# Scores, state update and state product of an mLSTM stage as float32 matmuls on two heads per 128 rows

## The chip, the cores and the metric

The kernel runs on one core of a Trainium2 chip. The metric is the device time of one execution in microseconds (us). The engines are TensorE (PE, with its weight loads PEld), VectorE (DVE), ScalarE (ACT), GpSimd (POOL) and SyncE (SP), whose queue issues nearly all transfers.

## What is computed

Three layers follow one another on 4 x 768 = 3072 tokens: an mLSTM recurrence with 8 heads of 40 numbers, a first dense layer of 2048 features with a leaky unit, and a second layer in which each token goes through one of 8 experts of 1024 features. All results are float32.

```python
for t in range(S):                                    # mLSTM, per batch and head
    m_new = np.maximum(f_gate[:, :, t] + m, i_gate[:, :, t])
    f_stab = np.exp(f_gate[:, :, t] + m - m_new); i_stab = np.exp(i_gate[:, :, t] - m_new)
    C = f_stab * C + i_stab * np.einsum('bhd,bhe->bhde', vt, kt)
    n = f_stab * n + i_stab * kt
    h_tilde = np.einsum('bhde,bhe->bhd', C, qt)
    denom = np.maximum(np.abs(np.einsum('bhd,bhd->bh', n, qt)[:, :, None]), 1.0)
    y[:, :, t] = o * h_tilde / denom                  # o = sigmoid(o_gate)
h = x @ w_in                                          # first layer, x is y with heads joined: 320 wide
x = (np.maximum(h, 0) + alpha * np.minimum(h, 0)) @ w_out
# second layer: expert_idx = argmax of normalised logits, then for each expert e
out[mask] = gate_w[mask, None] * (np.maximum(x[mask] @ w1[e], 0) @ w2[e])
```

## The kernel before

**The mLSTM works on 24 chunks** of 128 tokens (4 batches of 6). For each chunk `i` the kernel forms the scores of its tokens with each other (`a_s`, L433), weights and masks them (`a_mask`, `a_exp`, `a_p`), multiplies them by v and adds the product of q with the state left by the chunk before (`a_o`, L503), scales (`a_tot`, `a_y`, `a_yr`) and hands the result over, turned round by a transfer (`a_xt`, L564). The state of a head is 40 x 41 numbers (the last column is n). It is carried on by `a_u` (L440, a product of k and weighted v), `a_cd` (decay) and `a_c` (L478, the sum), for all but the last chunk of a batch.

**Float32 accuracy out of fp16 parts.** Before the change q, k, weighted v, the state and the weights are each cut into a high and a low fp16 part, and products are summed over parts. For q and k, `a_hi` (ACT), `a_qlo` and `a_klo` (DVE, L362 and L373) lay high and low parts side by side, so that a head fills 120 of 128 columns; `a_qt` and `a_kt` turn the 128 x 1024 fp16 arrays round with a transposing transfer each (`qT`, `kT`). A score is then one fp16 matmul per head (8 per chunk). The state update takes three fp16 matmuls per head (24 per chunk) and needs weighted v cut by `a_vwhi` and `a_vwlo`. The state is cut by `a_ct` (ACT) and `a_cs` (DVE, L496) before `a_o` multiplies it by q (8 matmuls per chunk, L513, beside 24 for scores times v, L514 to L516).

**The dense layers** lie around it. The products of the first layer are `m1` (L752, 16 matmuls a step) and `m2` (L840, 12 a step), on groups of one or two chunks; results of `m1` are drained by ACT (L759, L769), DVE (L765) and POOL (L772). Weights arrive as 64-bit floats and are turned into float32 bits on DVE (L642 to L646) and cut on ACT and POOL (L652 to L656). The weights of the second experts are cut in units (`ust`, `wo`, `wp`; L1150 to L1176) beside the first layer. The second layer (L1217, L1237) comes after.

**What sets the order.** All steps are entered in a plan with an engine, a rough cost and their predecessors; a list scheduler (`Plan.order`) puts them in one order, and three tables of numbers per kind of step (`LEAN`, `SOON`, `FIRST`) are added to the ranks. Each engine then runs its instructions in that order. The buffers `qs`, `ks`, `vs`, `xs` exist twice, scores and products share one two-bank PSUM tile (`SO`), so `a_s` of a chunk waits for `a_tot` of the chunk before.

Of the kernel before, what the change touches and what calls it, by code (L numbers as in the profile page):

```python
# [29 lines left out]
KST = 6 * D  # L30


def lean(k):
    # what a kind of step gets beyond its rank, and on top of it in the first chunks
    n = k[0]
    at = k[1] if len(k) > 1 and isinstance(k[1], int) else NCH
    return LEAN.get(n, 0.0) + (SOON.get(n, 0.0) if at < 4 else 0.0) + (FIRST.get(n, 0.0) if at < 2 else 0.0)


class Plan:  # L40
    """The order in which the steps are issued: a list schedule.  A step has an engine (T, V, A, G or S, the
    queue of the transfers), a rough cost, a rough transfer time, and the steps before it;
    of the steps that could start, the one with the most work behind it comes first."""
# [13 lines left out]
    def link(self, a, b, gap=0.0):  # L57
        # a goes before b as far as the ranks are concerned
        self.links.append((a, b, gap))

    def order(self):
# [8 lines left out]
        # ranks, from the last step back  # L70
# [22 lines left out]
        while any(ready.values()):  # L93
# [86 lines left out]
CHUNK = ("load", "mb", "mask0", "mask1", "exp0", "exp1", "exp2", "exp3", "hi", "qlo", "qt", "klo", "kt", "vhi", "vlo",  # L180
         "s", "p0", "p1", "phi0", "phi1", "plo0", "plo1", "vw", "vwhi", "vwlo", "u", "cd", "c", "ct", "cs", "o", "th",
# [4 lines left out]
def kernel(  # L186
    ctx: ExitStack,
    tc: tile.TileContext,
    qkvo: bass.AP,
# [22 lines left out]
    # ------------------------------------------------------------ constants  # L212
# [4 lines left out]
    # rows 0..79 hold high parts, 80..127 low parts (C); 0..63 / 64..127 (tails)  # L217
# [3 lines left out]
    sgnC = const.tile([P, 1], F32, name="sgnC")  # L221
    loC = const.tile([P, 1], F32, name="loC")
    V.tensor_scalar(loC, iot, 79.5, None, ALU.is_gt)
    V.tensor_scalar(sgnC, loC, -2.0, 1.0, ALU.mult, ALU.add)
# [11 lines left out]
    # ------------------------------------------------------------ gates  # L236
# [79 lines left out]
    # ------------------------------------------------------------ buffers  # L316
# [6 lines left out]
    qs = [att.tile([P, H, P], F16, name=f"qs{i}") for i in range(NB)]  # L323
    ks = [att.tile([P, H * KST + D], F16, name=f"ks{i}") for i in range(NB)]
    vs = [att.tile([P, 2, H, DV], F16, name=f"vs{i}") for i in range(NB)]
    xs = [att.tile([P, 6 * P], F16, name=f"xs{i}") for i in range(NB)]
    for i in range(NB):
        G.memset(qs[i][:, :, 3 * D:], 0.0)
        G.memset(ks[i][:, H * KST:], 0.0)
# [24 lines left out]
    def k6(i):
        return ks[i % NB][:, :H * KST].rearrange("p (h a d) -> p h a d", h=H, a=6)

    def a_hi(i):
        t = st["in", i]
        A.activation(qs[i % NB][:, :, 0:D], hd(t[:, 0]), AF.Copy, scale=64.0)
        A.activation(k6(i)[:, :, 0], hd(t[:, 1]), AF.Copy, scale=64.0)  # L360

    def a_qlo(i):  # L362
        t, q_ = st["in", i], qs[i % NB]
        V.scalar_tensor_tensor(q_[:, :, D:2 * D], hd(t[:, 0]), 64.0, q_[:, :, 0:D], ALU.mult, ALU.subtract)
        V.tensor_copy(q_[:, :, 2 * D:3 * D], q_[:, :, 0:D])

    def a_qt(i):
        q_ = qs[i % NB]
        qT = att.tile([P, H, P], F16, tag="qT", name="qT", bufs=2)
        SP.dma_start_transpose(out=qT, in_=q_.rearrange("p h d -> p (h d)"))  # L370
        st["qT", i] = qT

    def a_klo(i):  # L373
        t, k_ = st["in", i], k6(i)
        V.scalar_tensor_tensor(k_[:, :, 3], hd(t[:, 1]), 64.0, k_[:, :, 0], ALU.mult, ALU.subtract)
        V.tensor_copy(k_[:, :, 1:3], k_[:, :, 0:1].to_broadcast([P, H, 2, D]))
        kc = att.tile([P, H, P], F16, tag="kc", name="kc")
        kw = ks[i % NB][:, D:D + H * KST].rearrange("p (h d) -> p h d", h=H)
        V.tensor_copy(k_[:, :, 4:6], k_[:, :, 3:4].to_broadcast([P, H, 2, D]))  # L379
        V.tensor_copy(kc, kw[:, :, 0:P])  # L380
        st["kc", i] = kc

    def a_kt(i):
        kc = st.pop(("kc", i))
        kT = att.tile([P, H, P], F16, tag="kT", name="kT", bufs=1)
        SP.dma_start_transpose(out=kT, in_=kc.rearrange("p h d -> p (h d)"))
        st["kT", i] = kT

    def a_vhi(i):
        A.activation(vs[i % NB][:, 0, :, 0:D], hd(st["in", i][:, 2]), AF.Copy, scale=64.0)  # L390
# [1038 lines left out]
```

## Time and profile before

| | |
|---|---|
| median of 3 runs | 758.78 us (lowest 758.16, highest 760.66) |
| profiled execution, span from first to last instruction | 753.4 us |
| what lies around the span (758.78 - 753.4) | 5.4 us |
| PE busy, share of the span | 599.8 us, 80% |
| DVE busy | 558.0 us, 74% |
| POOL busy | 412.1 us, 55% |
| ACT busy | 392.4 us, 52% |

The share of busy time is a mean over stages that differ. In 40 slices of the span DVE stands at 9 tenths or near it until slice 27 and then falls to 1 or 2, while PE is nearly empty in the first four slices, at 7 or 8 after that, and at 9 from slice 27 on. So the span is read in stretches: a start of some 75 us, the stage in which chunks and the first layer run together until about 550 us, and the second layer.

### The profile page before, as it was taken

To read this page: it belongs to the slowest core of one execution; us is meant where nothing else is said; L and a number is where in the kernel's file an instruction comes from. 1 tells how busy PE (TensorE), PEld (TensorE's weight loads), DVE (VectorE), ACT (ScalarE), POOL (GpSimd) and SP (SyncE) were. 2 spreads that over 40 slices of the span, in tenths; PEclk is the share of its full clock that TensorE was granted. 3 is DMA by queue.
4 is the path that set the end of the run, shared out by engine and by line. 5 is a ranking of instruction groups with operands and counts; after the bars stand their busy time and mean duration, and the time that the engine had idled before them with its cause. 6 is when DMAs were issued, how large, how long until landed. Compare 5 with 4: busy or idle time off the path is not lost.

```text
span 753.4 us, 18492 instructions
## 1 busy us (share of the span) xinstructions
PE 599.8 (80%) x6941; PEld 493.9 (66%) x6941; DVE 558.0 (74%) x1278; ACT 392.4 (52%) x890; POOL 412.1 (55%) x487
## 2 busy tenths in 40 slices
PE   0023778788778888897888888799988999999995
PEld 0012666667566776685666766677777888888884
DVE  7899989999999999998999999989535212212111
ACT  3556766657777766786776776553221222222221
POOL 5858997767776546665566667462601333123322
PEclk9999789999899999999999999999999999999998
DMA  8897936489669968999899996625997699999893
GB/s 263 184 205 229 192 98 127 102 215 265 155 174 278 275 220 223 310 281 287 223 262 268 303 261 197 162 43 198 295 230 158 190 266 283 278 338 330 243 197 85
DMA packets 181551, 167.46 MB, mean 222 GB/s; under 512 B 122135, under 2 KB 158624, under 8 KB 177618
## 3 DMA queue, kind: packets, MB, share of 16 engines
q1 hardware_dynamic: 178178, 156.14, 79.0%
q0 software_dynamic: 3280, 10.10, 5.0%
q8 instruction: 56, 0.92, 0.5%
q14 instruction: 37, 0.30, 0.1%
HBM read 149.57 MB, written 30.26 MB: 239 GB/s over the span
## 4 chain that ended last, share of the span: by engine, by line
DVE 40%; DMA 31%; issue 11%; POOL 8%; PE 6%; ACT 3%; SPq 1%; POOLq 0%; DVEq 0%; ACTq 0%
DMA out_dram<-y,idx 16%; DVE r L765 7%; DMA x2t<-x2s 3%; DMA mb<-m_d 3%; DVE mb L457 2%; DMA wp<-wo 2%; POOL g L772 2%; PE hp L752 2%; DVE wo L1165 2%; DMA ust<-in_moe_w_dram 2%; POOL ph L467 2%; DMA wst<-in_moe_w_in_dram 2%; PE o L840 2%; DVE xs L560 2%; DVE ks L379 1%
## 5 line engine op out<-in xcount | busy, mean ns | idle before, releaser
L752 PE MATMUL hp<-xt,w_in_p 128*128 128x256 f16 (+1 forms) x1664 | 198.7, 279 | 26.0 <-DVE r L765 10.2
L752 PEld LDWEIGHTS <-w_in_p 128*128 128x128 f16 x1664 | 158.2, 104 | 50.8 <-DVE r L765 13.8
L840 PE MATMUL o<-w_out_p,g 128*128 128x320 f16 x1152 | 171.5, 303 | 8.5 <-ACT g L769 8.5
L772 POOL TENSOR_TENSOR g<-r,g 128x512 f16<-128x512 f32 (+1 forms) x104 | 130.3, 1259 | 81.2 <-ACT g L769 81.2
L840 PEld LDWEIGHTS <-g 128*128 128x128 f16 x1152 | 112.3, 99 | 52.4 <-ACT g L769 10.4
L1226 DVE SCALAR_TENSOR_TENSOR h<-hp,h 128x512 f16<-128x512 f32 x48 | 32.9, 689 | 112.8 <-ACT h L1222 112.7
L1243 POOL DMA_INDIRECT out_dram<-y,idx x27 | 27.3, 1011 | 132.5 <-ACT y L1240 61.1
L769 ACT ACTIVATE g<-r 128x512 f16<-128x512 f32 (+1 forms) x104 | 61.2, 592 | 73.5 <-DVE r L765 58.4
L765 DVE SCALAR_TENSOR_TENSOR r<-r,al,hp 128x256 f32<-128x256 f32 (+1 forms) x208 | 84.0, 449 | 2.5 <-ACT r L759 2.2
L1222 ACT ACTIVATE h<-hp 128x512 f16<-128x512 f32 x48 | 28.7, 597 | 94.3 <-PE hp L1217 92.1
L1237 PEld LDWEIGHTS <-h 128*128 128x128 f16 x648 | 61.9, 98 | 22.0
L467 POOL TENSOR_TENSOR ph<-mb,ph 128x512 f16<-128x512 f32 x48 | 64.3, 1344 | 19.3 <-ACT ph L463 19.2
L431 ACT ACTIVATE mb<-mb,aT 128x128 f32<-128x128 f32 x192 | 63.5, 390 | 10.7 <-POOL mb L424 10.4
L759 ACT ACTIVATE r<-hp 128x512 f32<-128x512 f32 (+1 forms) x104 | 57.0, 549 | 20.5 <-PE hp L752 13.9
L1217 PEld LDWEIGHTS <-wr 128*128 128x128 f16 x896 | 51.8, 98 | 1.4
L1217 PEld LDWEIGHTS <-w_in_p 128*128 128x128 f16 x832 | 49.3, 99 | 1.5
L1217 PE MATMUL hp<-xt,w_in_p 128*128 128x128 f16 x768 | 47.6, 221 | 0.0
L1217 PE MATMUL hp<-xt,wr 128*128 128x128 f16 x768 | 46.6, 219 | 0.0
L1237 PE MATMUL o<-wr,h 128*128 128x320 f16 x288 | 43.5, 302 | 0.0
L424 POOL TENSOR_SCALAR_AFFINE_SELECT mb<-mb 128x512 f32<-128x512 f32 x48 | 35.1, 751 | 14.8 <-DMA mb<-m_d 14.8
L1237 PE MATMUL o<-w_out_p,h 128*128 128x320 f16 x288 | 42.7, 299 | 0.0
L1192 POOL DMA_INDIRECT xg<-x_d,idx x31 | 30.4, 981 | 12.0 <-issue 8.4
(208 smaller groups left out, 1190.5 us busy)
## 6 DMA issues: line engine op xcount, KB each, us to landing
wr<-wp SPq DMA_DIRECT2D x32, 1280.0 KB
w_in_p<-wp SPq DMA_DIRECT2D x15, 1280.0 KB
w_out_p<-wp SPq DMA_DIRECT2D x15, 1280.0 KB
qkvo_t<-in_qkvo_dram SPq DMA_DIRECT2D x24, 640.0 KB
mb<-m_d SPq DMA_DIRECT2D x24, 512.0 KB
ust<-in_moe_w_dram SPq DMA_DIRECT2D x32, 320.0 KB
wp<-wo SPq DMA_DIRECT2D x32, 320.0 KB
ust<-in_moe_w_dram SPq DMA_DIRECT2D x16, 512.0 KB
```

The source lines that it names most:

```text
L424: G.affine_select(out=mb[:, sl], in_=mb[:, sl], compare_op=ALU.is_ge, fill=1.0e30, base=0, pattern=[[0, 4], [1, P]], channel_multiplier=-1)
L431: A.activation(mb[:, h], mb[:, h], AF.Exp, scale=-1.0, bias=aT[:, c, b * H + h:b * H + h + 1])
L467: G.tensor_tensor(st["P", i][:, 1, sl], st["mb", i][:, sl], st["P", i][:, 0, sl], ALU.subtract)
L752: T.matmul(hp[:, a, :n], lhsT=w_in_p[:, wk, f], rhs=xt[:, xk], start=z == 0, stop=z == 7)
L759: A.activation(r, e_t[j, m], AF.Relu, scale=-1.0)
L765: V.scalar_tensor_tensor(r[:, a], r[:, a], al1[:, m + a:m + a + 1], hp[:, a], ALU.mult, ALU.add)
L769: A.activation(g_t[j][:, 0, m:m + 2], e_t[j, m], AF.Copy)
L772: G.tensor_tensor(g_t[j][:, 1, m:m + 2], e_t.pop((j, m)), g_t[j][:, 0, m:m + 2], ALU.subtract)
L840: T.matmul(o[:, :DM], lhsT=g[:, gi, k, tt], rhs=w_out_p[:, k, a], start=z == 0, stop=z == 47)
L1217: T.matmul(hp[:, m], lhsT=w[:, wk, f], rhs=xt[:, xk], start=z == 0, stop=z == 7)
L1226: V.scalar_tensor_tensor(hs[:, 1], hp, 0.0, hs[:, 0], ALU.max, ALU.subtract)
L1237: T.matmul(o, lhsT=h[:, hi, k], rhs=w[:, k, a], start=z == 0, stop=z == 23)
```

## The change

Host code only lays out inputs: it now gives k padded to 64 columns per head beside v and the output gate (`kvo`), and a second array `qk_t` in which q and k are turned round already, two heads to 128 rows (head 2z in rows 0 to 39, head 2z+1 in rows 64 to 103, the rest zero).

- `a_hi`, `a_qlo`, `a_qt`, `a_klo`, `a_kt`, `a_vwhi`, `a_vwlo`, `a_ct`, `a_cs` are gone, and so are `qs` and `ks`.
- `a_loadt` is new: two transfers of 40 rows of 4 KB per chunk into one of three buffers `qk`, cleared once at the start (one on POOL, two on DVE).
- `a_s` is 8 float32 matmuls on 64 rows each, `a_u` 4 float32 matmuls of 128 x 82 on two heads at once, and the state product in `a_o` 4 float32 matmuls of 128 x 82 against a state `cf` (three buffers) that is zero outside the two heads' own blocks.
- `a_c` writes the state in two halves of 64 rows; `a_tot` is one multiplication of 328 columns where it was two of 164.
- Scores are held with even heads first, then odd ones, so `a_mb` is two transfers instead of one.
- The costs that the plan is given change with it; the three tables of numbers stay as they are.

```diff
+    qk = [att.tile([P, 2, H // 2, P], F32, name=f"qk{i}") for i in range(NQ)]
+    cf = [att.tile([P, H // 2, 2, DV], F32, name=f"cf{i}") for i in range(NST)]
+    def a_loadt(i):
+        x = qk[i % NQ].rearrange("p a h t -> p (a h t)")
+        for r in range(2):
+            SP.dma_start(x[64 * r:64 * r + D], qk_t[(2 * i + r) * D:(2 * i + r + 1) * D])
...
-    def a_klo(i):
-        t, k_ = st["in", i], k6(i)
-        V.scalar_tensor_tensor(k_[:, :, 3], hd(t[:, 1]), 64.0, k_[:, :, 0], ALU.mult, ALU.subtract)
-        V.tensor_copy(k_[:, :, 1:3], k_[:, :, 0:1].to_broadcast([P, H, 2, D]))
-        kc = att.tile([P, H, P], F16, tag="kc", name="kc")
-        kw = ks[i % NB][:, D:D + H * KST].rearrange("p (h d) -> p h d", h=H)
-        V.tensor_copy(k_[:, :, 4:6], k_[:, :, 3:4].to_broadcast([P, H, 2, D]))
-        V.tensor_copy(kc, kw[:, :, 0:P])
...
     def a_s(i):
-        for h in range(H):
-            T.matmul(sp[:, h], lhsT=kT[:, h], rhs=qT[:, h], start=True, stop=True)
+        x = qk[i % NQ]
+        for z in range(H // 2):
+            for r in range(2):
+                w = slice(64 * r, 64 * r + 64)
+                T.matmul(sp[:, r, z], lhsT=x[w, 1, z], rhs=x[w, 0, z], start=True, stop=True)
     def a_u(i):
-        for h in range(H):
-            T.matmul(up[:, h], lhsT=hi3, rhs=vwp[:, 0, h], start=True, stop=False)
-            T.matmul(up[:, h], lhsT=hi3, rhs=vwp[:, 1, h], start=False, stop=False)
-            T.matmul(up[:, h], lhsT=lo3, rhs=vwp[:, 0, h], start=False, stop=True)
+        for z in range(H // 2):
+            T.matmul(up[:, z], lhsT=k[:, z], rhs=vw[:, z], start=True, stop=True)
     def a_c(i):
-            V.scalar_tensor_tensor(cf, up, 2.0 ** -6, st["cd"], ALU.mult, ALU.add)
+        for r in range(2):
+            w = slice(64 * r, 64 * r + 64)
+                V.scalar_tensor_tensor(x, up[w, :, r], 64.0, st["cd"][w, :, r], ALU.mult, ALU.add)
     def a_o(i):
+            for z in range(H // 2):
+                T.matmul(op[:, 1, 2 * DV * z:2 * DV * (z + 1)], lhsT=qk[i % NQ][:, 0, z],
+                         rhs=cf[(i - 1) % NST][:, z].rearrange("p r d -> p (r d)"), start=True, stop=True)
-                T.matmul(inter, lhsT=qT[:, h], rhs=st["cs", i - 1][:, h], start=True, stop=True)
...
-        a("s", "T", 0.44, a_s, [("qt", i), ("kt", i), ("tot", i - 1)])
+        a("s", "T", 1.1, a_s, [("loadt", i), ("tot", i - 1)])
-            a("u", "T", 0.59, a_u, [("klo", i), ("vwlo", i), ("c", back)])
+            a("u", "T", 0.95, a_u, [("load", i), ("vw", i), ("c", back)])
-        a("o", "T", 0.79 if c else 0.59, a_o, [("plo0", i), ("plo1", i), ("vlo", i)] + ([("cs", i - 1)] if c else []))
+        a("o", "T", 1.5 if c else 0.59, a_o, [("plo0", i), ("plo1", i), ("vlo", i)] + ([("c", i - 1)] if c else []))
```

The first matmuls of chunks on PE, behind the transposes of the gates (`gps`). Before, the state update of the first chunk (`up`) opens, three fp16 matmuls per head, each with its weight load:

```order
L280 MATMUL gps<-ident,gates_b 128x32 x6
L299 MATMUL gps<-ident,gates_b 128x32 x10
L449 LDWEIGHTS ks_104
L449 MATMUL up<-vwp,ks_104 128x41
L450 LDWEIGHTS ks_104
L450 MATMUL up<-vwp,ks_104 128x41
L451 LDWEIGHTS ks_104
L451 MATMUL up<-vwp,ks_104 128x41
```

The same place after the change:

```order
L277 MATMUL gps<-ident,gates_b 128x32 x6
L296 MATMUL gps<-ident,gates_b 128x32 x10
L404 MATMUL sp<-qk_98 128x128 x8
L414 MATMUL up<-vw,kvo_t 128x82 x8
L463 LDWEIGHTS ph
L463 MATMUL op<-vs_101,ph 128x41
```

The scores (`sp`) of the first chunk now come first, since they wait for a load alone, and the updates of two chunks follow as 8 matmuls; a float32 matmul is one instruction that loads its own weights.

On DVE, one chunk's steps in the middle of the program (`cf` is the state, `qs` and `ks` the fp16 parts of q and k, `cs` those of the state, `kc` the copy that is transposed), before:

```order
L487 SCALAR_TENSOR_TENSOR cf<-up,cd 128x328
L364 SCALAR_TENSOR_TENSOR qs_103<-qkvo_t,qs_103 128x8x40
L365 COPY qs_103<-qs_103 128x8x40
L500 SCALAR_TENSOR_TENSOR cs<-cf,loC,ct 128x328
L375 SCALAR_TENSOR_TENSOR ks_105<-qkvo_t,ks_105 128x8x40
L376 COPY ks_105<-ks_105 128x8x80
L379 COPY ks_105<-ks_105 128x8x80
L380 COPY kc<-ks_105 128x1024
L909 SCALAR_TENSOR_TENSOR x2s_124<-o_4539,x2s_124 128x320
```

And after:

```order
L847 SCALAR_TENSOR_TENSOR x2s_124<-o_4023,x2s_124 128x320
L848 COPY x2s_124<-x2s_124 128x64
L450 SCALAR_TENSOR_TENSOR cf_106<-up,cd 64x4x41 x2
L867 TENSOR_SCALAR sc<-sc,tau_b 128x2
L868 RECIPROCAL sc<-sc 128x2
L703 SCALAR_TENSOR_TENSOR r<-r,al_122,hp 128x256 x2
```

Between the state sum and the next work of the dense layers seven instructions have gone; the sum itself is two.

On the SP queue at the start, where the first chunks' inputs are fetched (`wst` are weights of the first layer, `mb` the gate maxima), before:

```order
L350 DMA mb<-m_d 128x8x128
L307 DMA dec_d<-gates_b 32x4x1
L695 DMA wst<-in_moe_w_in_dram 128x1024 x2
L386 DMA_TRANSPOSE kT<-kc 128x8x128
L370 DMA_TRANSPOSE qT<-qs_102 128x8x128
```

And after:

```order
L349 DMA kvo_t<-in_kvo_dram 128x1152 x2
L272 DMA m_d<-gates_b 32x768
L355 DMA qk_98<-in_qk_t_dram 40x1024 x2
L355 DMA qk_99<-in_qk_t_dram 40x1024 x2
L633 DMA wst<-in_moe_w_in_dram 128x1024
```

What the scores wait for is issued right behind the first loads and no longer behind DVE work on the same chunk.

## Rows read from the trace of the kernel before

**Rows 1.** The page's first line: span and instructions.

```profile
span 753.4 us, 18492 instructions
```

**Rows 2.** Stretches: length, PE, PEld, DVE, ACT, POOL busy (instructions), granted clock, DMA, GB/s.

```profile
75.00:125.00 50.00, 37.47 (x478) 31.66 (x475) 46.12 (x109) 34.93 (x101) 46.64 (x51) 0.86 0.64 139
125.00:525.00 400.00, 337.10 (x3612) 269.72 (x3611) 383.08 (x871) 266.19 (x599) 249.32 (x301) 0.95 0.84 221
...
550.00:753.00 203.00, 190.14 (x2469) 164.33 (x2469) 50.66 (x133) 47.54 (x86) 52.39 (x53) 0.98 0.90 239
```

**Rows 3.** Groups of DVE, 125 to 525 us: count | busy us, mean ns | idle before.

```profile
L376 DVE COPY ks<-ks 128x640 f16<-128x640 f16 x18 | 12.5, 695 | 0.0
L500 DVE SCALAR_TENSOR_TENSOR cs<-cf,loC,ct 128x328 f16<-128x328 f32 x16 | 12.2, 764 | 0.3 <-ACT ct L494 0.3
...
L364 DVE SCALAR_TENSOR_TENSOR qs<-qkvo_t,qs 128x320 f16<-128x320 f32 x18 | 11.6, 646 | 0.0
...
L379 DVE COPY ks<-ks 128x640 f16<-128x640 f16 x18 | 10.5, 582 | 0.0
L380 DVE COPY kc<-ks 128x1024 f16<-128x1024 f16 x19 | 10.2, 539 | 0.7
L375 DVE SCALAR_TENSOR_TENSOR ks<-qkvo_t,ks 128x320 f16<-128x320 f32 x18 | 10.0, 557 | 0.0
...
L532 DVE TENSOR_TENSOR tot<-op,winT 128x164 f32<-128x164 f32 x34 | 9.4, 316 | 0.0
L365 DVE COPY qs<-qs 128x320 f16<-128x320 f16 x18 | 8.7, 485 | 0.0
...
L487 DVE SCALAR_TENSOR_TENSOR cf<-up,cd 128x328 f32<-128x328 f32 x12 | 5.8, 486 | 0.0
```

**Rows 4.** Waits of PE, 125 to 525 us: waited for: us, times, longest.

```profile
PE op L513 <- DVE cs L500: 10.0, 4, 3.6
PE hp L752 <- DVE r L765: 9.6, 9, 1.9
PE o L840 <- ACT g L769: 7.2, 4, 2.5
PE rp L1018 <- DVE oh L954: 6.7, 7, 2.3
PE lp L939 <- DMA x2t<-x2s: 6.4, 5, 3.2
...
PE hp L752 <- DVE sc L930: 4.0, 1, 4.0
PE sp L437 <- issue: 3.6, 2, 2.0
PE sp L437 <- DMA kT<-kc: 3.4, 2, 2.4
```

**Rows 5.** The chain that ended last, its start: start us, us, what.

```profile
41.98 1.28 DVE ks L379
...
47.29 7.36 DMA kT<-kc
...
62.10 1.00 DVE cs L500
```

**Rows 6.** PE in order of time: start us, us, instruction, count.

```profile
17.93 1.27 PE L299 MATMUL gps<-ident,gates_b 32*128 32x32 f32 x10 [9.80 <-ACT gates_b L293]
```

**Rows 7.** PE around 300 us: scores, products of the first layer, one state update.

```profile
300.85 0.61 PE L437 MATMUL sp<-qT,kT 128*128 128x128 f16 x8 [1.63 <-issue]
301.29 9.94 PE L840 MATMUL o<-w_out_p,g 128*128 128x320 f16 x72
311.07 0.18 PE L449 MATMUL up<-vwp,ks 128*128 128x41 f16 x1
...
311.65 0.18 PE L451 MATMUL up<-vwp,ks 128*128 128x41 f16 x1
```

**Rows 8.** One DVE line, whole span: shortest/median/longest ns.

```profile
L376 DVE COPY ks<-ks x24: 307/318/1804, 28.1 to 480.0; 128x640 f16<-128x640 f16 x24
```

More of the change, by code (lines that the diff above doesn't have):

```diff
@@ L188 @@
     tc: tile.TileContext,
[L189 removed]
+    kvo: bass.AP,
+    qk_t: bass.AP,
     i_gate: bass.AP,
@@ L383, in a_kt @@
[L383 to L387, printed above, removed]
     def a_vhi(i):
-        A.activation(vs[i % NB][:, 0, :, 0:D], hd(st["in", i][:, 2]), AF.Copy, scale=64.0)
+        A.activation(vs[i % NB][:, 0, :, 0:D], hd(st["v", i]), AF.Copy, scale=64.0)
     def a_vlo(i):
         v_ = vs[i % NB]
-        V.scalar_tensor_tensor(v_[:, 1, :, 0:D], hd(st["in", i][:, 2]), 64.0, v_[:, 0, :, 0:D],
+        V.scalar_tensor_tensor(v_[:, 1, :, 0:D], hd(st["v", i]), 64.0, v_[:, 0, :, 0:D],
@@ L482, in a_c @@
         up = st.pop(("U", i))
-        cf = att.tile([P, H, DV], F32, tag="cf", name="cf", bufs=2)
-        if c == 0:
-            A.activation(cf, up, AF.Copy, scale=2.0 ** -6)
-        else:
-            V.scalar_tensor_tensor(cf, up, 2.0 ** -6, st["cd"], ALU.mult, ALU.add)
-        st["C"] = cf
-    def a_ct(i):
-        if i % NC_ == NC_ - 1:
-            return
-        st["ct"] = att.tile([P, H, DV], F16, tag="ct", name="ct")
-        A.activation(st["ct"], st["C"], AF.Copy, scale=sgnC)
-    def a_cs(i):
-        if i % NC_ == NC_ - 1:
-            return
-        cs = att.tile([P, H, DV], F16, tag="cs", name="cs", bufs=2)
-        V.scalar_tensor_tensor(cs, st["C"], loC, st["ct"], ALU.mult, ALU.add)
-        st["cs", i] = cs
+        for r in range(2):
+            w = slice(64 * r, 64 * r + 64)
+            x = cf[i % NST][w, :, r]
+            if c == 0:
+                A.activation(x, up[w, :, r], AF.Copy, scale=64.0)
+            else:
+                V.scalar_tensor_tensor(x, up[w, :, r], 64.0, st["cd"][w, :, r], ALU.mult, ALU.add)
     def a_o(i):
@@ L578, in a @@
                        if not (len(d) == 2 and isinstance(d[1], int) and d[1] < 0)])
[L580 to L582 removed]
+        a("load", "S", 0.06, a_load, [(n, i - 3) for n in ("th", "vlo")]
+          + ([("u", i - 3)] if (i - 3) % NC_ < NC_ - 1 else []), dma=1.7)
+        a("loadt", "S", 0.12, a_loadt, [(n, i - NQ) for n in ("s", "o")], dma=1.0)
+        a("mb", "S", 0.12, a_mb, [("g_store",), ("plo0", i - 2), ("plo1", i - 2)], dma=1.46)
         for j in range(2):
@@ L1404, in layout, with rows @@
     d = dict(inputs)
-    tok = [np.asarray(inputs[n]).transpose(0, 2, 1, 3).reshape(NT, DM) for n in ('q', 'k', 'v', 'o_gate')]
-    d['qkvo'] = np.concatenate(tok, axis=1)
+    def rows(n):
+        return np.asarray(inputs[n]).transpose(0, 2, 1, 3).reshape(NT, DM)
+    kp = np.zeros((NT, H, KW), np.float32)
+    kp[:, :, :D] = rows('k').reshape(NT, H, D)
+    d['kvo'] = np.concatenate([kp.reshape(NT, H * KW), rows('v'), rows('o_gate')], axis=1)
+    qk = np.stack([np.asarray(inputs[n]) for n in ('q', 'k')]).reshape(2, B, H // 2, 2, NC_, P, D)
+    d['qk_t'] = qk.transpose(1, 4, 3, 6, 0, 2, 5).reshape(NCH * 2 * D, 2 * H // 2 * P)
     d['i_gate'] = np.asarray(inputs['i_gate']).reshape(B * H, S)
```

154 lines of the change are left out of this document (53 added, 101 removed).

## Prediction

> **What bounds the kernel now.** I read the page's first line and its slices, then the engines' busy time by stretches, then the waits of PE in the long middle stretch, and last the chain of work that ended last. The profiled execution spans 753.4 us [rows 1]; the median is 758.78 us, so 5.4 us lie around the span, and I add them at the end. The slices show three stages. Up to 75 us PE has hardly begun. From 75 to 125 us DVE works 46.1 and POOL 46.6 of 50 us, PE 37.5. From 125 to 525 us DVE works 383.1 of 400 us, 96%, and PE 337.1, so PE stands idle for 62.9 us. From 550 us on PE works 190.1 of 203 us and everything else is light [rows 2]. Two conclusions: the second layer is PE's own, and nothing that leaves the chunks can shorten it; the middle is set by DVE, but PE is only 62.9 us behind. Taking work from DVE therefore buys at most those 62.9 us, less whatever PE is given to do. That is the heart of the case: DVE loses much, PE gains some, and PE is next.
>
> **What goes from DVE.** In the middle stretch seven groups disappear (the low parts and copies of q and k and the state's parts): 12.5 + 12.2 + 11.6 + 10.5 + 10.2 + 10.0 + 8.7 = 75.7 us [rows 3]. The state sum becomes two instructions of 164 columns; the row of that width took 316 ns against 486 ns for the whole, so 12 x (2 x 0.316 - 0.486) = +1.8 us; the two multiplications of `tot` become one, about 17 x 0.486 = 8.3 us in place of 9.4 us [rows 3]. DVE goes from 383 to some 308 us. It stops being the bound by a wide margin; even if PE filled the stretch without a gap it would need more.
>
> The copies also show how far a mean can be trusted: the shortest of the `ks` copies took 307 ns, the median 318, the longest 1804, and the mean was 695 [rows 8, 3]. More than half of that line's time is waiting within the instruction. The Trainium skill (SBUF — State Buffer, "SBUF: two separate sides") says that DVE and GpSimd share a pair of ports as an exclusive lock, held for a whole instruction. The spread of the row agrees with it, and by that rule some of the waiting would not vanish but move to whatever DVE runs next: with half of the 75.7 us staying, DVE would be at 346 us, and I would count half instead of two thirds of its waits below as gone, 3.4 us less gain.
>
> **What PE gets.** Per chunk, before: 8 scores in 0.61 us with the tail of the last; 24 state updates that start within 0.58 us, 0.025 us apart; and 8 of the same size for the state product, about 0.2 us [rows 7]. After: 8, 4 and 4 float32 matmuls. The trace shows no float32 product, only float32 transposes: ten, each with a 128-column load, in 1.27 us, so 0.127 us each [rows 6]. This bounds the cost from both sides. *Low end*, one such step each: scores 1.02 us (+0.41), update 0.51 us (-0.25 against 0.76 with its tail), product 0.51 us (+0.31). The stretch holds 19 chunks with scores (`kc` x19), 16 with an update (`cs` x16) and 17 with a state product (`tot` x34, two each) [rows 3]: 7.8 - 4.0 + 5.3 = +9 us. *High end*, four such steps for each, nothing overlapping: scores +3.45, update +1.27, product +1.83 us, so 65.6 + 20.3 + 31.1 = +117 us. I take +30 us: the plan's costs for the new steps are 1.1, 0.95 and 1.5 us; its old costs 0.44, 0.59 and 0.79 agree with the pace of the rows (24 x 0.025 = 0.60 for the update, 8 scores 0.61 with the tail), so I read the new ones on the same scale; 19 x 0.66 + 16 x 0.36 + 17 x 0.71 = 12.5 + 5.8 + 12.1 = 30.4 us. That is nearer to the low end, and I keep both ends for the range.
>
> The Trainium skill (FP8 and Floating Point Precision, "TensorE Precision Notes") says that a true float32 product takes four passes through the array. No row here shows a float32 product. As an estimate by that page, with the pace of `m2` (9.94 us / 72 / 320 = 0.43 ns per column, [rows 7]), four passes stream 8 x 4 x 128 columns in 1.76 us and 4 x 4 x 82 in 0.57 us; that makes +31 us in the stretch if the loads are hidden, and the high end if each pass loads anew. So the rule does not choose between my value and the slower rival; it makes the low end unlikely.
>
> **What becomes of PE's 62.9 us.** The waits for `cs` (10.0), for `kT` (3.4) and the queue wait before the scores (3.6) have no cause any more: 17.0 us gone [rows 4]. In place of `cs` the product waits for the state sum, two steps earlier in the same chain. The waits for DVE's own pieces of the dense layers, 9.6 + 6.7 + 4.0 = 20.3 us [rows 4], shrink with its queue; I take two thirds, 13.5 us. The waits for `g` on ACT and for the transfer `x2t` (7.2 + 6.4 us) come behind DVE work too, but also behind their own; I take a quarter, 3.4 us. Together -34 us, leaving 29 us idle. The granted clock averages 0.95 here [rows 2]; at levels of 2.4 and 1.2 GHz that is a tenth of 400 us at the lower one, 20 us of lost work; in the stretch before, where PE works a smaller share, it is 0.86 [rows 2]. With under half of the waits left I take back 8 us. Sum of the middle stretch: -34 + 30 - 8 = -12 us.
>
> **The start.** On the chain of the first 75 us stand a copy of `ks` (1.28 us), the transposing transfer of `kT` (7.36 us) and a `cs` (1.00 us) [rows 5], 9.6 us of steps that are gone; the scores now wait for a load issued behind the first ones on SP. What is next late is POOL, 46.6 of 50 us busy from 75 us on [rows 2]: it drains `m1` and cuts weights, so I give nothing beyond the 9.6 us. Against it stand the clears of `qk` and `cf`: they lie ahead of the clear that the gate scan waits for, about 1 us on POOL by the `kc` row (0.54 us for 1024 fp16 columns) [rows 3]; the two on DVE are covered by the scan's own wait. The added SP issues (three per chunk) replace two transposing ones and delay nobody. ACT loses work too, but it does not set the middle stretch (266 of 400 us) [rows 2]. Start: -9 us.
>
> **Sum.** -9 - 12 = -21 us on the span, 753.4 to 732.4; with 5.4 us around it, **738 us**.
>
> **Rivals.** *A. PE pays too much (slower).* The place is PE's queue in the middle stretch: a float32 matmul that loads and streams four times, with nothing overlapping, stands in order ahead of `m1` and `m2`. The relief above is 9 + 34 + 8 = 51 us, so it decides from 51 us added, or 2.7 us per chunk (51 / 19). At the high end, +117 us, the kernel would take 758.8 + 66 = 825 us; at three steps each, scores +2.44, update +0.76, product +1.32, so 46 + 12 + 22 = +80 us, 788 us. For it: the float32 transposes run at 0.127 us where fp16 pairs run at 0.025. Against it: the plan's costs, and scores on two halves of the rows, which need not exclude each other. Chance 0.20. *B. The idle time closes almost wholly and the float32 work costs its low end:* -9 - 45 + 9 - 10 = -55 us, 704 us. For it: DVE would have 90 us to spare. Against: one pass for a float32 product. Chance 0.13. *C. PE's waits are not DVE's load but the order,* written with three tables of numbers that name steps which no longer exist: only the 17.0 us with a removed cause go, and no clock is regained: -9 - 17 + 30 = +4 us, 763 us, no change or a little slower (752 to 768). For it: each listed wait is 1 to 5 us long, at 1 to 9 places, as a missed order looks. Against: DVE is busy 96% around them. Chance 0.12.
>
> **How the numbers follow.** The forecast (722 to 752 us) has 0.55, A 0.20, B 0.13, C 0.12. The measurement can tell 0.3%, some 2.3 us, from no change. Faster: nearly all of the forecast (0.52), B (0.13), part of C (0.05): 0.70. Same: 0.03 of the forecast, 0.04 of C: 0.07. Slower: A and the rest of C: 0.23. The range leaves out the lower part of B (0.08) and the upper part of A (0.12): 712 to 780 us.
>
> **What would show it.** In the trace after: DVE near 310 us in a stretch of the same work, PE above 90% in it; groups of float32 `sp`, `up` and `op` whose starts give 1.1, 0.95 and 0.9 us a chunk; no PE wait named `cs` or `kT`; scores of the first chunk some 10 us earlier; the granted clock above 0.95; the second layer as long as before. The forecast is wrong if a chunk's float32 work takes over 4.5 us of PE in all, if PE still waits 50 us in the middle for DVE, ACT or POOL, or if the second layer starts no earlier although DVE has gone quiet.

## The result, and the profile after

| | before | after |
|---|---|---|
| median of the runs made side by side | 759.72 us (4 runs) | 771.49 us (4 runs, 768.91 to 772.14) |
| ratio, 95% interval | | 1.0148 (1.0103 to 1.0193) |
| span of the profiled execution | 753.4 us [rows 1] | 767.2 us |

The changed kernel is slower, by 11.8 us; the forecast was 738 us, so the direction was wrong: the median moved by 1.5%, clear of the noise. The new time lies beyond rival C (the order, 763 us, at most 768), whose chance had been put at 0.12.

The page of the kernel after, its first line and its busy time by engine (busy, share of the span, instructions):

```profile
span 767.2 us, 17926 instructions
PE 633.8 (83%) x6813; PEld 527.6 (69%) x6813; DVE 474.7 (62%) x1110; ACT 361.2 (47%) x806; POOL 379.4 (49%) x467
```

DVE lost 558.0 - 474.7 = 83.3 us of work, PE gained 633.8 - 599.8 = 34.0 us. Both are close to what was foreseen, and yet the kernel is slower. The stretches of the kernel after, as in [rows 2] (length, busy time of PE, PEld, DVE, ACT, POOL with instructions, granted clock, DMA share, GB/s):

```profile
25.00:50.00 25.00, 5.18 (x40) 4.52 (x40) 10.36 (x23) 10.69 (x28) 12.23 (x12) 1.00 0.70 149
125.00:525.00 400.00, 349.61 (x3399) 284.36 (x3399) 301.45 (x696) 237.34 (x525) 223.50 (x280) 0.95 0.73 201
```

Three marks split the loss of 13.8 us in the span. The first product of the first layer (`m1`) starts at 67.7 us before and at 71.8 us after, that of the second layer at 553.2 and 570.8 us. So the start is 4.1 us longer, the part from there to the second layer 13.5 us (485.5 to 499.0), and the rest 3.8 us shorter (200.2 to 196.4).

In the middle stretch no engine is busy throughout any more. PE stands idle for 400 - 349.6 = 50.4 us, where it was 62.9 before; the granted clock is still 0.95. What PE waits for there, beside [rows 4] (engine, line, what ended the wait: us in total, times, longest):

```profile
PE op L458 <- DVE cf L450: 18.6, 6, 4.4
PE lp L877 <- DMA x2t<-x2s: 12.2, 7, 3.2
PE rp L956 <- DVE oh L892: 5.8, 2, 3.2
PE op L465 <- POOL ph L427: 5.1, 6, 1.2
PE hp L690 <- DVE r L703: 4.6, 2, 2.7
```

The waits for `cs`, `kT` and the queue are gone and those for `r` and `oh` smaller. But the state product now waits 18.6 us for the state sum `cf`, where it waited 10.0 us for `cs`, and `x2t` takes 12.2 us, where it took 6.4. The float32 matmuls themselves, PE in order of time from 300 to 330 us (start us, us, instruction, records):

```profile
301.35 1.02 PE L414 MATMUL up<-vw,kvo_t 128*128 128x82 f32 x8
303.83 1.03 PE L458 MATMUL op<-cf,qk 128*128 128x82 f32 x8
308.65 1.16 PE L404 MATMUL sp<-qk 64*128 64x128 f32 x16
```

A chunk's scores take 1.16 us, its update 1.02 and its product 1.03; from the start of each group to the start of the next instruction it is 1.10, 0.85 and 0.86 us. The first row is the update of the chunk before: it stands shortly ahead of the product that needs it. Here the fold of the state lay on ACT (the first chunk of a batch) and PE did not wait. One of the six waits for DVE's fold reads so, first PE, then DVE:

```profile
335.00 1.02 PE L414 MATMUL up<-vw,kvo_t 128*128 128x82 f32 x8
341.94 1.97 PE L458 MATMUL op<-cf,qk 128*128 128x82 f32 x8 [4.18 <-DVE cf L450]
```

```profile
335.44 4.38 DVE L1103 SCALAR_TENSOR_TENSOR wo<-ust,wo 128x640 f16<-128x640 f32 x3
...
341.14 0.66 DVE L450 SCALAR_TENSOR_TENSOR cf<-up,cd 64x164 f32<-64x164 f32 x2
```

The update ends at 336.0 us. DVE is then busy with weights of the second experts (`wo`) and other work of the dense layers, and folds the state only from 341.1 us on. In which place a step stands in its engine's queue is a question of the order. The wait costs PE more than its own length: the product behind it takes 1.97 us in place of 1.02, and the granted clock from 341 to 344 us is 0.50, the lower level (1.2 GHz), where it was 1.00 from 335 to 341.

The start changed too. Before, the same 25 us from 25 to 50 us read:

```profile
25.00:50.00 25.00, 4.55 (x80) 3.96 (x80) 21.77 (x34) 12.79 (x32) 17.50 (x16) 1.00 0.88 171
```

DVE works 10.4 us in place of 21.8. Of these 11.4 us, 8.0 are steps that the change removed (`ks`, `qs`, `kc` and `cs` in this window), as intended. The rest of the loss is the conversion of weights `w` from 64-bit floats, which falls from 13.8 to 7.4 us. Its groups in the window, before and after (count | busy us, mean ns | idle before):

```profile
L644 DVE SCALAR_TENSOR_TENSOR w<-wst,w 128x512 int32<-128x512 int32 x6 | 5.8, 1011 | 0.0
L642 DVE TENSOR_SCALAR w<-wst 128x512 int32<-128x512 int32 (+1 forms) x5 | 4.2, 864 | 3.2 <-POOL ttl L656 3.2
L646 DVE SCALAR_TENSOR_TENSOR w<-wst,w 128x512 int32<-128x512 int32 x6 | 3.8, 676 | 0.0
```

```profile
L582 DVE SCALAR_TENSOR_TENSOR w<-wst,w 128x512 int32<-128x512 int32 x4 | 2.6, 680 | 0.0
L584 DVE SCALAR_TENSOR_TENSOR w<-wst,w 128x512 int32<-128x512 int32 x4 | 2.6, 679 | 0.0
L580 DVE TENSOR_SCALAR w<-wst 128x512 int32<-128x512 int32 x4 | 2.2, 579 | 2.7 <-DMA wst<-in_moe_w_in_dram 2.7
```

Why the conversion is late is seen on SP's queue, first of the kernel before, then of the kernel after (start us, us, engine line operation):

```profile
11.16 8.24 SPq L695 DMA_DIRECT2D wst<-in_moe_w_in_dram  x5
...
23.86 1.33 SPq L897 DMA_TRANSPOSE enp<-ep  x1
...
29.06 0.91 SPq L695 DMA_DIRECT2D wst<-in_moe_w_in_dram  x2
```

```profile
12.49 2.92 SPq L633 DMA_DIRECT2D wst<-in_moe_w_in_dram  x3
...
26.01 1.33 SPq L835 DMA_TRANSPOSE enp<-ep  x1
...
31.24 7.41 SPq L633 DMA_DIRECT2D wst<-in_moe_w_in_dram  x4
```

Five loads of the weights that DVE turns into float32 went out in this window ahead of the transposing transfer of the expert embedding, and two behind it at 29.06 us; after, three did, and four stand behind it and behind transfers into `w_in_p`, issued over 7.4 us from 31.24 us on. DVE's next conversion begins at 41.29 us.

### The profile page after: what moved, and what is told of

Same layout as the page of the kernel before. It is cut to its first block, busy times and chain, and to the rows that moved or that the text cites. A ratio compares the mean times of both kernels' runs of the same rounds, so it can differ in the third digit from the quotient of the medians.

```text
span 767.2 us, 17926 instructions
## 1 busy us (share of the span) xinstructions
PE 633.8 (83%) x6813; PEld 527.6 (69%) x6813; DVE 474.7 (62%) x1110; ACT 361.2 (47%) x806; POOL 379.4 (49%) x467
## 4 chain that ended last, share of the span: by engine, by line
PE 39%; DVE 27%; DMA 15%; ACT 7%; issue 6%; POOL 2%; SPq 2%; POOLq 0%; DVEq 0%; ACTq 0%
PE hp L1155 11%; PE o L1175 9%; PE o L778 9%; DVE r L703 6%; PE hp L690 6%; DMA x2t<-x2s 4%; DMA mb<-m_d 4%; DVE wo L1103 3%; ACT mb L395 2%; DVE w L580 2%; DMA out_dram<-y,idx 2%; DVE w L582 2%; DVE mb L419 2%; DMA ust<-in_moe_w_dram 2%; DMA decB<-dec_d 1%
## 5 line engine op out<-in xcount | busy, mean ns | idle before, releaser
L690 PE MATMUL hp<-xt,w_in_p 128*128 128x256 f16 (+1 forms) x1664 | 193.8, 274 | 13.8 <-DMA xt<-xs 6.8
L690 PEld LDWEIGHTS <-w_in_p 128*128 128x128 f16 x1664 | 155.7, 102 | 36.4 <-DVE r L703 7.9
L710 POOL TENSOR_TENSOR g<-r,g 128x512 f16<-128x512 f32 (+1 forms) x104 | 120.4, 1164 | 78.2 <-ACT g L707 77.8
L427 POOL TENSOR_TENSOR ph<-mb,ph 128x512 f16<-128x512 f32 x48 | 66.0, 1390 | 20.1 <-ACT ph L424 19.9
L386 POOL TENSOR_SCALAR_AFFINE_SELECT mb<-mb 128x512 f32<-128x512 f32 x48 | 31.6, 679 | 52.0 <-DMA mb<-m_d 51.8
L1155 PEld LDWEIGHTS <-w_in_p 128*128 128x128 f16 x832 | 47.0, 98 | 0.9 <-issue 0.3
L1178 ACT ACTIVATE y<-o,xg 128x320 f32<-128x320 f32 x24 | 12.7, 527 | 69.9 <-PE o L1175 60.6
L414 PE MATMUL up<-vw,kvo_t 128*128 128x82 f32 x160 | 25.2, 310 | 23.9 <-DVE cf L450 12.4
L1155 PE MATMUL hp<-xt,w_in_p 128*128 128x128 f16 x768 | 44.1, 219 | 0.1
L1155 PE MATMUL hp<-xt,wr 128*128 128x128 f16 x768 | 43.9, 219 | 0.0
L1103 DVE SCALAR_TENSOR_TENSOR wo<-ust,wo 128x640 f16<-128x640 f32 x32 | 37.3, 1177 | 7.5 <-ACT wo L1093 7.4
```

Source lines behind the costliest of these rows:

```text
L427: G.tensor_tensor(st["P", i][:, 1, j], st["mb", i][:, j], st["P", i][:, 0, j], ALU.subtract)
L690: T.matmul(hp[:, a, :n], lhsT=w_in_p[:, wk, f], rhs=xt[:, xk], start=z == 0, stop=z == 7)
L710: G.tensor_tensor(g_t[j][:, 1, m:m + 2], e_t.pop((j, m)), g_t[j][:, 0, m:m + 2], ALU.subtract)
L1103: V.scalar_tensor_tensor(w[:, :, 1], t, 512.0, w[:, :, 0], ALU.mult, ALU.subtract)
L1155: T.matmul(hp[:, m], lhsT=w[:, wk, f], rhs=xt[:, xk], start=z == 0, stop=z == 7)
```

## The experiments

The theories. **O, the order:** the three tables hold numbers fitted to the old steps. They hold the state update back by 57.3 us (`u` in `LEAN`); the entry of +25.0 that drew `cs` forward has no step any more, and other entries move SP's first loads. The change itself is worth a gain that this order hides. **P, the passes:** the float32 matmuls hold PE for longer than DVE's relief gives back. Later runs ask what the passes and DVE's time are worth once the order is out of the way. All ratios are to the kernel before, run beside each kernel (medians of 759.5, 758.4 and 759.6 us in the three groups of runs).

| kernel | median us | ratio (95% interval) |
|---|---|---|
| after, one pass (`e1_one_pass`) | 765.23 | 1.0081 (1.0043 to 1.0119) |
| after, state early (`e2_state_early`) | 758.06 | 0.9969 (0.9945 to 0.9993) |
| after, state early and loads early (`e8_state_start`) | 749.18 | 0.9863 (0.9798 to 0.9927) |
| after, only `LEAN` (`e9_lean_only`) | 760.58 | 1.0022 (0.9987 to 1.0057) |
| after, tables empty (`e5_after_flat`) | 749.72 | 0.9867 (0.9810 to 0.9923) |
| after, empty but state early (`e7_flat_state`) | 743.40 | 0.9777 (0.9706 to 0.9848) |
| the same and five more entries (`e13_more_entries`) | 748.35 | 0.9844 (0.9809 to 0.9879) |
| before, tables empty (`e4_before_flat`) | 778.32 | 1.0233 (1.0194 to 1.0273) |
| before, empty but state early (`e12_before_state`) | 766.26 | 1.0094 (1.0070 to 1.0119) |
| `e5_after_flat` with one pass (`e6_flat_one_pass`) | 746.59 | 0.9817 (0.9744 to 0.9890) |
| `e7_flat_state` with one pass (`e10_state_one_pass`) | 739.38 | 0.9745 (0.9698 to 0.9792) |
| `e7_flat_state` with DVE work put back (`e11_dve_back`) | 801.34 | 1.0528 (1.0475 to 1.0580) |

### The passes taken away

```diff
+    def top(ap):
+        return ap.bitcast(BF)[..., 1::2]
...
-                T.matmul(sp[:, r, z], lhsT=x[w, 1, z], rhs=x[w, 0, z], start=True, stop=True)
+                T.matmul(sp[:, r, z], lhsT=top(x[w, 1, z]), rhs=top(x[w, 0, z]), start=True, stop=True)
```

The update and the product are changed in the same way. It leaves out the lower 16 bits of each number, so this is a probe and no kernel to use.

> The changed kernel with its float32 matmuls (scores, state update, state product) reading only the upper 16 bits of each number, as bfloat16: one pass instead of two, lower accuracy, same order of steps, same plan costs. Theory P (PE became the bound, and the float32 passes are what the kernel lost): PE busy falls by about 2 us a chunk, some 40 us of the 634, and the time falls with it by 30 us or more, to 742 us or less. Theory O (the order of steps makes PE wait; the passes fill time in which it would have waited anyway): PE's idle time grows instead and the time falls by 15 us at most, to 756 us or more.

765.23 us: P falls, and O holds. ("Two" passes in the expectation are the two records that a float32 matmul leaves in the trace, 8 for the 4 matmuls of an update above; with 16-bit operands the 4 leave 4. The trace does not count passes.) The middle stretch of this kernel and its longest wait on PE:

```profile
125.00:525.00 400.00, 331.09 (x3173) 256.62 (x3170) 308.68 (x734) 239.77 (x532) 222.99 (x281) 0.93 0.74 205
```

```profile
PE op L462 <- DVE cf L454: 27.9, 8, 4.9
```

PE works 18.5 us less than after and waits that much more; the wait for `cf` went from 18.6 to 27.9 us and the granted clock from 0.95 to 0.93. Over the whole span PE is busy 38.1 us less (633.8 to 595.7), and the time is 5 to 6 us shorter: most of what was taken from PE came back as waiting.

### The state first

```diff
+LEAN.update(u=25.0, c=25.0)
+FIRST.update(u=0.0, c=0.0)
```

> The changed kernel with the state update and state sum raised in the tables of the plan (from -57.3 and -3.7 to 25 each, and their extra for the first chunks set to zero), as the removed step that cut the state had it. Theory O: PE's wait of the state product for the state sum, 18.6 us in six waits in the middle stretch, falls below 8 us and the time by 5 to 15 us. Theory P: the wait falls too, but PE has no less to do and waits elsewhere; the time stays within 3 us of 771 us.

758.06 us, 13 us below the changed kernel. PE's waits from 125 to 525 us no longer name `cf` at all; the longest are

```profile
PE lp L879 <- DMA x2t<-x2s: 10.6, 4, 4.1
PE op L467 <- POOL ph L429: 10.3, 11, 1.6
PE sp L406 <- issue: 5.7, 3, 3.7
```

Drawing two kinds of step forward undoes the whole loss: O holds for the middle. Which of the two it takes was not told apart.

### The tables emptied, in both kernels

```diff
+LEAN, SOON, FIRST = {}, {}, {}
```

> The kernel before with its three tables of numbers emptied, so that the list scheduler goes by ranks alone. Theory O (the tables fit the old steps and not the new ones): the kernel before loses 10 us or more by it, 770 us or more. Theory P: the tables matter little, under 5 us, and the loss of the change is PE work.

> The changed kernel with the three tables emptied, the partner of the kernel before with emptied tables. Theory O: it is no slower than that partner (the loss of 12 us was the tables' fit), and near 771 us, since the tables no longer fitted. Theory P: it is again 10 to 15 us slower than its partner.

778.32 us for the old steps, 749.72 us for the new ones. Without the tables the old kernel loses 19 us, and the new one wins 22. The sign turns: under one and the same rule the change takes 778.3 to 749.7 us, -28.6 us. The two kernels' waits of PE for the state, from 125 to 525 us, first the old steps and then the new:

```profile
PE op L514 <- DVE cs L501: 36.6, 9, 7.2
```

```profile
PE op L459 <- DVE cf L451: 7.4, 5, 3.6
```

The fitted tables had brought the first of these to 10.0 us [rows 4]; on the new steps they made 18.6 us out of 7.4. O had the second kernel near 771 us; that it came out so far below was not foreseen.

### Which table does the harm

> The changed kernel with the table for all chunks kept and the two further tables for the first four and first two chunks emptied. It tells whether the harm sits in the start or in the middle. Theory M (the middle: the state's update held back by 57.3 us in every chunk): the wait of the state product for the state stays at 15 us or more, and the time is 760 to 775 us. Theory S (the start): the time falls most of the way to the 749.7 us with all three emptied, 750 to 757 us.

```diff
+SOON, FIRST = {}, {}
```

760.58 us, within theory M's bounds, with 21.8 us of waiting for `cf` from 125 to 525 us: M holds. Yet 10.9 us lay in the tables for the first chunks (771.5 to 760.6), about half of the loss, and as much in the table for all chunks (760.6 to 749.7).

### The start

```diff
+LEAN.update(u=25.0, c=25.0, pload=0.0)
+FIRST.update(u=0.0, c=0.0)
```

> The changed kernel with its tables but for two things: the state's update and fold go first (that alone gave 758.1 us), and the loads of the first expert's w_in are no longer held back by 6.6 us, so that SP issues two of them ahead of the transposes of the expert embedding instead of at 31.2 us. Theory S (the changed kernel's start is late because DVE waits for those loads, 11.4 us less DVE work than before between 25 and 50 us, and m1 starts 4.1 us later): 4 to 8 us less than 758.1 us, and DVE busy 15 us or more between 25 and 50 us. Theory N (the start is hidden by PE's later waits or the wait moves to another load): 755 to 761 us.

749.18 us, 8.9 us less than the state alone by the medians, some 8 by the ratios, so at the upper bound of S. The two profiled executions differ by 5.2 us (758.0 to 752.8), and by the same 5.2 us `m1` starts earlier (71.3 to 66.1). Its start:

```profile
25.00:50.00 25.00, 5.17 (x40) 4.53 (x40) 15.79 (x28) 11.11 (x29) 15.39 (x14) 1.00 0.70 160
```

And SP's queue there:

```profile
...
18.61 0.45 SPq L635 DMA_DIRECT2D wst<-in_moe_w_in_dram  x1
26.00 1.34 SPq L837 DMA_TRANSPOSE enp<-ep  x1
```

DVE works 15.8 us there instead of 10.4, and the conversion of weights is back at 13.8 us: a fourth load now stands ahead of the transposing transfer. With the fitted tables and three entries changed (`u`, `c`, `pload`) the new steps stand where empty tables put them.

### Empty tables with the state first

```diff
+LEAN, SOON, FIRST = {"u": 25.0, "c": 25.0}, {}, {}
```

> The changed kernel with the three tables emptied but for two entries of 25 us, which let the state's update (PE) and its fold (DVE) go first among the steps that stand ready. Theory O: the wait of the state product for the state (7.4 us between 120 and 540 us with empty tables) is the one wait on PE in the middle that the order still makes at the state; it goes, and the time falls by 2 to 7 us below the 749.7 us with empty tables. Theory N (empty tables are as good as it gets and each entry only moves a wait): 748 to 756 us, with the wait for the state gone and another one grown by as much.

```diff
+LEAN, SOON, FIRST = {"u": 25.0, "c": 25.0, "ct": 25.0, "cs": 25.0}, {}, {}
```

> The kernel before with its three tables emptied but for entries of 25 us that let the state's steps (update, fold and the two that make the state's fp16 parts) go first: the same rule that gave the changed kernel 743.4 us, and 778.3 us with empty tables. It gives the change's worth with neither order fitted. Theory O (each kernel's order decides, and the change itself is worth 15 to 30 us): 760 to 775 us, the wait for cs much smaller than 44.6 us. Theory F (a few entries do as well as the fitted tables in either kernel, and the change is worth less): 745 to 758 us.

The new steps take 743.40 us, faster than both kernels of the case and 6.3 us less than with empty tables, as O had it; no wait for `cf` is left from 125 to 525 us. The old steps take 766.26 us under the same rule, within O's bounds, and no wait for `cs` is left there either. The middle of the two kernels, old steps and then new:

```profile
125.00:525.00 400.00, 338.55 (x3587) 269.51 (x3584) 381.78 (x857) 262.71 (x597) 248.15 (x300) 0.94 0.84 215
```

```profile
125.00:525.00 400.00, 370.51 (x3608) 300.86 (x3607) 318.67 (x767) 245.48 (x537) 233.66 (x290) 0.96 0.77 215
```

PE's idle time goes from 61.5 to 29.5 us, near the forecast's 62.9 to 29, and the time falls by 22.9 us, against the 21 of the forecast's sum. So the relief of the middle is there, and the tables hid it. That the sums agree is luck all the same. The marks of the two executions, first products of the first and of the second layer, old steps and then new (ns shortest/median/longest, first and last start in us):

```profile
L753 PE MATMUL hp<-xt,w_in_p x1664: 216/273/421, 54.0 to 540.5; 128*128 128x256 f16 x156, 128*128 128x128 f16 x29
L1218 PE MATMUL hp<-xt,wr x768: 217/219/229, 555.7 to 711.6; 128*128 128x128 f16 x192
```

```profile
L691 PE MATMUL hp<-xt,w_in_p x1664: 216/273/421, 60.1 to 517.3; 128*128 128x256 f16 x156, 128*128 128x128 f16 x29
L1156 PE MATMUL hp<-xt,wr x768: 216/219/314, 532.9 to 692.3; 128*128 128x128 f16 x192
```

The first layer starts 6.1 us later with the new steps (7.1 us later with empty tables alone, 51.9 to 59.0), the part from there to the second layer is 28.9 us shorter (501.7 to 472.8), and the rest of the spans of 761.4 and 741.1 us is 2.5 us longer. The forecast had -9, -12 and 0. And the waits that are left are others than it had left: for `xt` (9.7 us), `ph` (7.0) and `sc` (7.2 in two rows).

> The changed kernel with empty tables, the state's update and fold first (743.4 us), and besides the fp16 parts of the masked scores (which the product waits for: 7.0 us between 120 and 540 us, 8.2 us before) and the load of q and k 10 us ahead of their rank. Theory G (there is more to be had by the order): 736 to 741 us, the waits for ph at half or less. Theory N (a wait that goes comes back elsewhere): 741 to 748 us.

```diff
+LEAN, SOON, FIRST = {"u": 25.0, "c": 25.0, "phi0": 10.0, "phi1": 10.0, "plo0": 10.0, "plo1": 10.0, "loadt": 10.0}, {}, {}
```

748.35 us, 5 us more than without the entries and just above N's bounds: G falls. PE's wait for POOL's `ph` from 125 to 525 us is 8.1 us in place of 7.0, and no smaller. Drawing the steps of `ph` forward did not bring it sooner here.

### What the float32 passes cost, and what DVE's time is worth

> The changed kernel with its three tables emptied (749.7 us in the run of that alone), and besides with the float32 operands of scores, update and product read as their upper 16 bits, so that each product is one pass on TensorE; nothing else of the order or of the planned costs is touched, and the values are rounded to 8 bits. Theory O (the order holds the changed kernel up, and the passes are paid in full only where PE has no gaps): with most of PE's gaps gone, the passes taken away (1.64 us in each of 18 chunks of the middle stretch, 48 us per chunk set in all, some 29 us of PE's busy time in the middle against the kernel before) should now show, at half or more: 722 to 737 us. Theory P (the matmuls are hidden by what PE waits for in either order): no change within 5 us, 745 to 755 us.

> The changed kernel with empty tables and the state's update and fold first (743.4 us in the run of that alone), and the float32 operands of scores, update and product read as their upper 16 bits, so that each is one pass; the values are rounded to 8 bits. With empty tables alone the one pass was worth 3 us, while the product's waits for the state rose from 7.4 to 18.8 us. Theory W (that wait swallowed the passes taken away): with the state first it is gone, and 10 us or more show: 725 to 734 us. Theory H (the passes lie in time in which PE would have waited for DVE, ACT and POOL anyway, whichever of them is late): 737 to 745 us, PE's idle time in the middle up by 15 us or more.

746.59 against 749.72 us, so O of the first of these falls and P holds, and 739.38 against 743.40 us. By the ratios the passes are worth 0.0050 and 0.0032, 2 to 4 us, and in the first experiment 0.0067, 5 us; the intervals of each pair overlap, so the size is uncertain by several us, but 20 to 30 us it is not. Over the whole span PE is busy 38.9 us less in the second pair (635.1 to 596.2). All three pairs keep the order and the planned costs of the float32 kernel; whether an order made for the shorter products would gain more was not run. The waits tell where the time went: with the state first, one pass has PE wait for the low part of the weights that POOL cuts, first the kernel with four-byte operands, then the one with one pass, its stretch and its wait (125 to 525 us):

```profile
PE op L466 <- POOL ph L428: 7.0, 7, 1.4
```

```profile
125.00:525.00 400.00, 348.96 (x3358) 272.23 (x3356) 319.57 (x767) 243.10 (x535) 236.24 (x289) 0.93 0.77 217
```

```profile
PE op L470 <- POOL ph L432: 23.1, 20, 2.1
```

PE works 21.6 us less in the same 400 us, 16.1 us of that come back in this one wait, and the granted clock falls from 0.96 to 0.93. H holds, and W with its 10 us or more falls.

```diff
+    def a_spare(i):
+        k = st["k", i]
+        for _ in range(6):
+            V.scalar_tensor_tensor(spare, k, 64.0, k, ALU.mult, ALU.subtract)
...
+            a("spare", "V", 4.1, a_spare, [("load", i)])
-            a("u", "T", 0.95, a_u, [("load", i), ("vw", i), ("c", back)])
+            a("u", "T", 0.95, a_u, [("load", i), ("vw", i), ("c", back), ("spare", i)])
```

> The same kernel (empty tables, state first, 743.4 us) with DVE work put back: in each chunk that updates the state six operations over 128x512 float32 with a float16 result (about 0.6 us each by the 0.69 us of the second layer's), written to a tile that nobody reads, ahead of the update as the splits of k stood in the kernel before. It puts back some 4 us of DVE per chunk, about what the change took away (383 to 301 us in the stretch from 125 to 525 us). Theory D (the change's gain is DVE's time): 755 us or more. Theory T (the gain is the shorter chains and the DMA transposes that are gone, and DVE has room for the work): 742 to 748 us.

801.34 us. The line that was put back, from the page (busy us, mean ns | idle before), and who stands in the chain that ended last:

```profile
L379 DVE SCALAR_TENSOR_TENSOR spare<-kvo_t 128x512 f16<-128x512 f32 x120 | 119.2, 993 | 3.4
DVE 51%; PE 26%; DMA 10%; issue 7%; POOL 2%; ACT 2%; SPq 1%; POOLq 0%; DVEq 0%; ACTq 0%
```

119.2 us of DVE work cost 801.34 - 743.40 = 57.9 us, 0.49 us for each; DVE has 51% of the chain, where it has 28% without the work. By the bounds D holds and T falls. But the dose was larger than meant: at 993 ns apiece it is 119.2 us, where the change took away 83.3, and where DVE stood idle for 106 us of the 533 ahead of the second layer in the kernel without the work. The work also stands in front of the update, and the plan was told of it, so the order moved too. PE's waits in the middle do not name it or the state: the longest are for `r` (13.9 us), `ph` (11.3) and `oh` (8.8). So DVE, though idle a fifth of the middle stretch without the work, can't take this much for nothing; whether some 80 us would have found room stays open. How the 23 to 29 us of the change divide between DVE's time, the shorter chains and the DMA transposes that are gone was not told apart: 83.3 us at 0.49 would be 41 us, more than the change gave, so the price of the work put back is not that of the work removed.

## Why the prediction went wrong, step by step

- **What goes from DVE: right.** 83.3 us are gone from the whole span; I had 75 us in the middle stretch. The doubt drawn from the Trainium skill (SBUF — State Buffer, "SBUF: two separate sides"), by which waiting inside instructions would move to the next ones, did not decide: DVE stood at 301 us, not at 346, in the stretch. Over the whole span the groups that went had 100 us, and those that stayed came out the same in sum, some longer (the `wo` pieces of 128 x 640 from 977 to 1177 ns), some shorter.
- **What PE gets: right as busy time, wrong as a price.** Per chunk, from the start of a group to the start of the next instruction, 1.10 - 0.44 = +0.66, 0.85 - 0.61 = +0.24 and 0.86 - 0.20 = +0.66 us; with 19, 16 and 17 of them 12.5 + 3.8 + 11.2 = +27.6 us, against +30.4. But this term went into the sum in full, and the runs with one pass put it at 2 to 5 us. In a stretch where PE has gaps a us of PE was not a us of the kernel. The Trainium skill (FP8 and Floating Point Precision, "TensorE Precision Notes") gives four passes for a true float32 product, from which I had estimated +31 us. The sum agrees, its parts do not: the scores took 1.10 us where the estimate had 1.76, the update and the product 0.85 and 0.86 where it had 0.57 each. The trace shows two records for each float32 matmul, so it doesn't show the count of passes.
- **What becomes of PE's 62.9 us: this step failed.** Forecast -34 us of waiting and -8 of clock; it was 50.4 - 62.9 = -12.5 us and nothing. The sentence that failed is "In place of `cs` the product waits for the state sum, two steps earlier in the same chain": being earlier in the chain is of no use to a step whose start a table holds back. The wait became 18.6 us, not less than 10.0. The wait for `x2t`, of which a quarter was to go, grew from 6.4 to 12.2 us. From `m1` on to the second layer the kernel took 13.5 us more, where the forecast had 12 less. With `u` and `c` drawn forward the wait was gone, and with empty tables besides the stretch had 29.5 us idle, as much as forecast.
- **The start, -9 us: failed.** It was +4.1 us. I cut the removed steps from the chain and said that the added SP issues delay nobody. I had not asked whether the loads on SP keep their places; two of them moved behind a transposing transfer, and DVE converted 6.4 us less of weights from 25 to 50 us. One entry more (`pload`) gave 5 to 9 us. The tables are not all of it: the first layer starts 6 to 7 us later with the new steps under a neutral order too. The first scores did come earlier, by 23 us (41.6 to 18.5), but `m1` waits for the turned result of a chunk (`xt`), which comes long after its scores. Which step ahead of `xt` is later with the new steps was not taken apart.
- **The second layer, 0: right.** From its first product on it takes 200.2 us before and 196.4 after. The loss of 13.8 us in the span is all ahead of it.
- **The rivals.** A: 3.2 us of float32 work per chunk, where it needed 2.7 us more than before and the rows give 1.6; it did not happen. Its price came from float32 transposes at 18 us, where float32 work is slower than later: in the kernel after the same 8 scores took 2.08 us at 18.5 us and 1.16 at 308.7. B did not happen either: even in the best of the orders run 29.5 us stay idle. C was the cause, and too cheap: it counted only waits without a cause as gone and let the others stay, at 763 us. It had no place for a new wait, nor for the start. The argument against it, that DVE is busy 96% around the waits, was true of before and said nothing of after, where DVE is busy 75%. The text itself had the point for C in hand, that the tables name steps which no longer exist, and gave it 0.12.
- **Its own signs.** One sign of being wrong came true: the second layer starts no earlier, although DVE has gone quiet. Waits for DVE, ACT and POOL were 35.2 of the 50.4 us, under the 50 that it had named.

What was argued only: that the tables are fitted to the old steps is read from what they do (19 us gained on the old, 22 lost on the new); how they came about the trace can't tell. Which part of the harm of `SOON` and `FIRST` lies in which entry was not taken apart beyond `pload`, `u` and `c`.

## What to carry to other kernels

Where a table or hand-written order sets the places, a change that removes, renames or re-costs steps is two changes: run it once with the order neutral in both kernels, before judging either. When an edit takes work from the full engine, what it is worth is the relief less what the order does with it: list the entries that name steps touched, and the wait that each would make. And work on an engine with gaps is worth what is left after its waits have changed: here some 20 us of PE work taken out of the middle stretch, 39 us out of the span, gave 2 to 5 us. An agreeing total is no proof of the parts: here -21 was forecast and -22.9 measured, from parts that were off by 15 and 17 us.

## What the runs showed of the hardware that was not expected

- A float32 matmul leaves two matmul records. 8 of 64 x 128 take 1.16 us and 4 of 128 x 82 take 1.02 us with the tail of the last, where 24 fp16 matmuls of an update took 0.76. With 16-bit operands (`e10_state_one_pass`) the same 8 and 4 take 0.40 and 0.32 us.
- Early on PE is slower, and the granted clock does not show it: in the kernel after, the 8 float32 scores take 2.08 us at 18.5 and at 52.2 us and 1.16 at 308.7 us, and the granted clock of 15 to 25, 50 to 60 and 300 to 312 us reads 1.00 each time. In the middle a product as slow (1.97 us at 341.9) comes with a granted clock of 0.50. What slows PE at the start no row shows.
- The operation put back on DVE has a median of 693 ns, but a mean of 993 and a longest of 4708 ns: 30% of its time lies above the median. The longest runs from 144.90 to 149.61 us, while POOL works without a gap from 144.92 to 149.67 us. Both its inputs are in SBUF; by the Trainium skill (SBUF — State Buffer, "SBUF: two separate sides") such an operation and one of GpSimd that reads SBUF shut each other out for a whole instruction. The trace agrees with it as far as these times go.

The shortest, median and longest time of that line over the whole span:

```profile
L379 DVE SCALAR_TENSOR_TENSOR spare<-kvo_t x120: 673/693/4708, 14.2 to 464.2; 128x512 f16<-128x512 f32 x120
```

- Taking work from PE lowered its granted clock each time: 0.95 to 0.93, 0.97 to 0.93 and 0.96 to 0.93 in the middle stretch of the three pairs. How much of the time that did not fall is due to this was not measured.
